# Top-k attention and mixture of experts: the count comparison of the kth score moves from VectorE to GpSimd

## The chip, the core and the metric

The kernel runs on one core of a Trainium2 chip. Its engines are TensorE (PE, with its weight loads as PEld), VectorE (DVE), ScalarE (ACT), GpSimd (POOL) and SyncE (SP, which here issues DMAs). The metric is the time of one execution on the device, in microseconds (us). The kernel before takes 1193.73 us, the median of three runs (1190.71 to 1193.77).

## The reference

```python
# attention: 8 batches, 8 heads, 576 rows, head size 64
scores = scale * np.matmul(q, k.transpose(0, 1, 3, 2))
kth = np.partition(scores, -top_k, axis=-1)[..., -top_k:-top_k + 1]     # top_k = 32
mask = scores >= kth
scores = np.where(mask, scores, -1000000000.0)
attn = np.exp(scores - np.max(scores, axis=-1, keepdims=True))
attn = attn / (np.sum(attn, axis=-1, keepdims=True) + 1e-09)
x = np.matmul(attn, v)                      # then 4608 rows of 512
# experts: 8 of 512 -> 1024 -> 512, one per row
logits = x @ w_gate + modality_bias[modality_id]
e_idx = np.argmax(logits, axis=1)
gate_w = softmax(logits)[np.arange(N), e_idx]
out[mask] = gate_w[mask, None] * (np.maximum(x[mask] @ w1[e], 0.0) @ w2[e])
```

For each row of 576 scores the 32nd largest one (`kth`) is needed, before the exponentials of the scores at or above it are kept.

## The kernel before

**Tiles and steps.** The 64 heads are taken in 32 pairs of 9 tiles of 128 rows by 576 scores: 288 tiles. The main loop (`for i in range(LAST)`, L1123) is a software pipeline. Step i works on tile i in one stage, on tile i - 1 in the next, and so on, and beside it TensorE gets a share of the expert matmuls for batches that are already routed.

**The stages of a tile.** TensorE makes the scores (`qk`, L384), ScalarE copies them to SBUF as `Ssb` (L389). VectorE takes the 8 largest of each of six pieces of 96 (`cand`, L396), and in the next step the 24 largest of these 48 (`chain`, L407 to L409, into `mg`). GpSimd turns the 24th into a threshold (`below`, `n`, L421). ScalarE takes the sign of each score against it (`sign`, `K`, L428) and, in the accumulator of the same instruction, a count that tells how many scores are larger; the count goes to `n[:, 0, x]`. GpSimd multiplies scores and signs (`pool_y`, `y`, L434), one step behind `sign`, and one step behind that VectorE takes the 8 largest of `y` (`find`, L438) into the last places of `mg`.

**The pick.** For three tiles at once, in every third step, `pick` (L440) gives VectorE three small instructions. `eq` (L445) compares the three counts with nine constants `i9s`, giving ones and zeros in 3 x 9; `jk` (L446) multiplies `eq` with nine candidate values of `mg`; `kth` (L447) adds up, so that the one candidate that fits the count is left. Then VectorE masks: `keep` (`P`, L458), one instruction that compares with `kth`, multiplies with the exponentials `ex` and sums the row. For two of three tiles of the first 48 tiles it is split: VectorE makes a mask (`hide`, `hT`, L465), GpSimd adds it to the scores (`hidden`, L471, whose output has the name `ex`), ScalarE takes the exponential (`masked`, L477).

**What sets the order.** VectorE's order inside a step comes from `arrange` (L949), a small planner with a cost, a delay and an earliest time for each kind of work (`USE`, `FROM`, L27 and L28). GpSimd's order is that of the calls in the loop: in a step `hidden` (if there is one), `gate` (L481, one element of `P` read, so that what follows waits for the mask of the step before), `pool_y`, in one step of nine `fill` (L346, two instructions), scatters of routed rows (`DMA_INDIRECT`, L611 and L826, when there are any), `below` (`n`), and in one step of three `small` (`sm`, L415).

Of the kernel before, what the change touches and what calls it, by code (L numbers as in the profile page):

```python
# [9 lines left out]
FT = mybir.dt.float32  # L10
# [4 lines left out]
OP = mybir.AluOpType  # L15
# [25 lines left out]
LY = KL + 2  # L41
LT = LY + 1
# [35 lines left out]
def kernel(  # L78
# [13 lines left out]
    V, A, G, PE, SP = nc.vector, nc.scalar, nc.gpsimd, nc.tensor, nc.sync  # L92
# [21 lines left out]
    wk = att.enter_context(tc.tile_pool(name="wk", bufs=3))  # L114
# [6 lines left out]
    LD, PR, T = {}, {}, {}  # L121
# [55 lines left out]
    def fiota(name, shape, pattern, base, cm):  # L177
        t = const.tile(shape, FT, name=name)
        G.iota(t, pattern=pattern, base=base, channel_multiplier=cm, allow_small_or_imprecise_dtypes=True)
        return t  # L180

    i9s = fiota("i9s", [128, 3, 9], [[0, 3], [2, 9]], S - 2 * TOPK, 0)
# [160 lines left out]
    def fill(p, bd):  # L343
        for h in range(2):
            r = slice(h * 64, h * 64 + 64)
            G.tensor_scalar(bd[r, :, r], PR[p]["st"][r, :, 1, 512:].bitcast(FT), 1.0, 1.0, op0=OP.mult, op1=OP.mult)  # L346
# [84 lines left out]
    def pool_y(i):  # L431
        t = T[i]
        t["y"] = wk.tile([128, S], FT, name="y", bufs=YB)
        G.tensor_tensor(t["y"], t["S"], t["K"], op=OP.mult)  # L434

    def find(i):
        t = T[i]
        V.max(t["mg"][:, i % 3, 24:32], t["y"])  # L438

    def pick(i):  # L440

        t = T[i]
        eq, v = (wk.tile([128, 3, 9], FT, name=nm, bufs=1) for nm in ("eq", "jk"))
        n = t["n"][:, 0, :]
        return [lambda: V.tensor_tensor(eq, i9s, n[:, :, None].to_broadcast([128, 3, 9]), op=OP.is_equal),  # L445
                lambda: V.tensor_tensor(v, eq, t["mg"][:, :, 23:32], op=OP.mult),  # L446
                lambda: V.tensor_reduce(kth[:, i - 2:i + 1], v, axis=AX.X, op=OP.add)]  # L447

    def expo(i):
# [281 lines left out]
    def expert(s, act, nxt, whole, defer):  # L731
# [111 lines left out]
        if nxt:  # L843
            pick, rows, done, tok = sched(s + 1, whole)
            todo = pick + done + rows + tok
            c, k = len(todo) - 2, (2 if whole else 3) * (1 + o["xt"])
            cut = [min(k * x, c) for x in range(CUT[0])] + [c + 1] * (CUT[1] - CUT[0]) + [c + 2]

            def both(f, a, b):
                f()  # L850
                chore.extend(todo[a:b])
                if not defer:
                    chores()
            n = len(cut) - 1
            return [(c, lambda f=f, a=a, b=b: both(f, a, b), w) for (c, f, w), a, b in zip(main, cut, cut[1:])] + main[n:]
# [14 lines left out]
    def ready(n, whole):  # L870
        pick, rows, done, tok = sched(n, whole)
        for f in pick + done + rows + tok:
            f()
        for g in range(4):
            load_w1(n, g)
        for g in range(4):
            load_w2(n, g)
# [13 lines left out]
    def more_moe():  # L891
# [14 lines left out]
        elif full >= n + 1:  # L906
            now = SL[n - 1] if moe else {"xt": True, "used": [4, 4]}
            if not now["xt"]:
                return
            plan.update(ready=n, go=False)  # L910
            pick, rows, done, tok = sched(n, fits(n))
            free = []

            def begin():
                free.extend(now["used"])
                now["nxt"] = True

            def take(x, g):
                return lambda: weight(lambda: (load_w1, load_w2)[x](n, g)) if g < free[x] else None
            l1 = [take(0, g) for g in range(4)]  # L920
            l2 = [lambda: [take(1, g)() for g in range(4)]]
            go = [lambda: plan.update(go=True)]
            if n == 0:
                held = [lambda: [held_.popleft()() for _ in range(len(held_))]]

                def sent():

                    while sends:
                        sends.popleft()()
                rush.extend(pick + [begin] + done + [PAUSE, sent] + rows + l1[:2] + [PAUSE] + go + held + [l1[2], l1[3], PAUSE, PAUSE] + tok + l2)  # L930
            else:
                begun, rest = ([], go) if moe else (go, [])
                rush.extend(pick + [begin] + rows + rest + l1[:1] + done + [PAUSE, l1[1], l1[2], PAUSE, l1[3]] + l2 + begun + [PAUSE] + tok)
# [8 lines left out]
    def run(kind, fs, *after):  # L942

        ops = []
        for f in fs:
            ops.append(Op(kind if isinstance(kind, str) else kind[len(ops)], f, *(ops[-1:] or after)))
        return ops
# [175 lines left out]
    for i in range(LAST):  # L1123
# [138 lines left out]
        ops, found, got = [], None, None  # L1262
# [5 lines left out]
        if ok(i - LT):  # L1268
            found = Op("find", lambda: find(i - LT))
            ops.append(found)  # L1270
            if (i - LT) % 3 == 2:
                e_, v_, s_ = pick(i - LT)
                e_ = Op("pick", e_)
                v_ = Op("pick", v_, e_, found)
                got = Op("pick", s_, v_)
                ops += [e_, v_, got]
        ops += run("late", lo)
        small_ = []
        quick = 0 <= b1 < FAST and r < 16
# [27 lines left out]
            gate(i - 1 - LR)  # L1307
        if ok(i - LY):
            pool_y(i - LY)
        if j == 4 and p + 1 < NPAIR:  # L1310
            fill(p + 1, qbd[(p + 1) % 2])
        for x in puts:
# [13 lines left out]
        if i == CLOSE:  # L1326
# [7 lines left out]
            wk = att.enter_context(tc.tile_pool(name="tl", bufs=1))  # L1334
# [53 lines left out]
    wk = att.enter_context(tc.tile_pool(name="wkb", bufs=3))  # L1388
# [101 lines left out]
```

## Time and profile before

| what | value |
|---|---|
| median of three runs | 1193.73 us (1190.71 to 1193.77) |
| profiled execution, its own time | 1191.36 us |
| its span | 1189.7 us |
| PE busy | 1150.4 us (97%) |
| DVE busy | 1089.2 us (92%) |
| ACT busy | 981.5 us (83%) |
| POOL busy | 670.6 us (56%) |
| chain that ended last | PE 64%, DVE 23%, ACT 6% of the span |
| granted TensorE clock, mean of the span | 0.995 |

Busy time is the union of an engine's instruction spans. The chain is followed back from the last instruction, at each step to what released it. Attention fills the time to about 1008 us; expert matmuls alone follow.

### The profile page before, as it was taken

How to read it: one execution, taken by the hardware profiler on the slowest of the kernel's cores; microseconds unless marked ns; L12 is line 12 of the kernel's file. 1: busy time of each engine (PE TensorE's matmuls, PEld its weight loads, DVE VectorE, ACT ScalarE, POOL GpSimd, SP SyncE). 2: the span in 40 equal slices, each digit the busy share in tenths (PEclk: the TensorE clock that was granted, in tenths of full speed). 3: DMA queues.
4: the chain of work that ended last, by engine and by line, in shares of the span. 5: the costliest groups of instructions: out<-in, count | busy, mean ns of one | idle time of the engine just before them, and what ended most of it. 6: DMA issues, size and time to landing. Idle time of an engine off the chain costs nothing.

```text
span 1189.7 us, 28032 instructions
## 1 busy us (share of the span) xinstructions
PE 1150.4 (97%) x7902; PEld 904.1 (76%) x7902; DVE 1089.2 (92%) x5474; ACT 981.5 (83%) x2015; POOL 670.6 (56%) x1256
## 2 busy tenths in 40 slices
PE   8889979999999999999999999999999999999998
PEld 6667768777777868777686877778687777589987
DVE  7999999999999999999999899999999999476762
ACT  5999979998889979998999899989999887355653
POOL 6888875555656565566566566557655665221111
PEclk9999999999999999999999999999999999999999
DMA  5663357653677368654785448664765554287750
GB/s 125 161 183 90 89 164 221 191 151 87 169 221 199 86 178 241 170 151 129 199 244 156 129 134 242 168 163 133 204 185 134 173 145 148 71 288 250 245 191 22
DMA packets 204323, 197.09 MB, mean 166 GB/s; under 512 B 104413, under 2 KB 151533, under 8 KB 204160
## 3 DMA queue, kind: packets, MB, share of 16 engines
q1 hardware_dynamic: 196880, 175.92, 53.4%
q0 software_dynamic: 6080, 19.00, 4.4%
q8 instruction: 66, 1.08, 0.4%
q14 instruction: 97, 0.79, 0.2%
q10 hardware_dynamic: 1200, 0.30, 0.1%
HBM read 118.63 MB, written 24.23 MB: 120 GB/s over the span
## 4 chain that ended last, share of the span: by engine, by line
PE 64%; DVE 23%; ACT 6%; issue 2%; DMA 2%; POOL 1%; SPq 0%; POOLq 0%; ACTq 0%; DVEq 0%
PE E L798 11%; PE E L811 11%; PE X L520 10%; PE S L384 8%; PE T L492 7%; DVE cand L396 6%; PE X L1085 5%; PE X L1069 4%; DVE mg L438 4%; DVE P L458 4%; PE E L1069 1%; PE X L318 1%; ACT K L428 1%; ACT Ssb L389 1%; DVE cand L407 1%
## 5 line engine op out<-in xcount | busy, mean ns | idle before, releaser
L396 DVE MAX8 cand<-Ssb 128x8 f32<-128x96 f32 x1728 | 389.5, 245 | 2.1 <-ACT Ssb L389 2.1
L434 POOL TENSOR_TENSOR y<-Ssb,K 128x576 f32<-128x576 f32 x288 | 368.2, 1279 | 8.9 <-ACT K L428 8.6
L428 ACT ACTIVATE K<-Ssb,n 128x576 bf16<-128x576 f32 x288 | 230.0, 799 | 9.2 <-POOL y L434 9.0
L384 PE MATMUL S<-ks,qs 128*128 128x288 f32 x992 | 222.7, 346 | 9.9 <-ACT Ssb L389 6.5
L389 ACT ACTIVATE Ssb<-S 128x576 f32<-128x576 f32 x284 | 187.9, 662 | 53.5 <-PE S L384 32.4
L438 DVE MAX8 mg<-y 128x8 f32<-128x576 f32 x288 | 213.4, 741 | 3.9 <-POOL y L434 3.9
L798 PE MATMUL E<-xgT,w1b 128*128 128x256 f32 x832 | 201.2, 384 | 3.5 <-ACT hT L802 1.6
L452 ACT ACTIVATE ex<-Ssb,sm 128x576 f32<-128x576 f32 x256 | 202.9, 793 | 0.0
L500 ACT ACTIVATE PT<-T 128x640 f32<-128x640 f32 (+1 forms) x288 | 193.6, 672 | 6.7 <-PE T L492 6.6
L811 PE MATMUL E<-w2b,hT 128*128 128x512 f32 x416 | 195.8, 597 | 0.5 <-ACT hT L802 0.2
L384 PEld LDWEIGHTS S<-ks,qs 128*128 128x128 f32 x992 | 152.9, 190 | 56.8 <-issue 26.0
L458 DVE SCALAR_TENSOR_TENSOR P<-Ssb,kth,ex 128x576 f32<-128x576 f32 x230 | 191.3, 832 | 3.0 <-ACT ex L452 1.7
L492 PE MATMUL T<-idf,P 128*128 128x128 f32 x1152 | 169.6, 274 | 6.3 <-ACT P L477 5.3
L798 PEld LDWEIGHTS E<-xgT,w1b 128*128 128x128 f32 x832 | 150.8, 190 | 30.0 <-ACT hT L802 6.6
L481 POOL TENSOR_SCALAR spare<-P 1x1 f32<-1x1 f32 x230 | 41.9, 182 | 211.7 <-DVE mg L407 175.0
L492 PEld LDWEIGHTS T<-idf,P 128*128 128x128 f32 x1152 | 137.6, 141 | 12.5 <-ACT P L477 8.8
L520 PE MATMUL X<-PT,vm 128*64 128x256 f32 (+1 forms) x1536 | 145.2, 331 | 1.0 <-ACT xgT L757 0.5
L520 PEld LDWEIGHTS X<-PT,vm 128*64 128x64 f32 x1536 | 87.7, 137 | 45.3 <-issue 10.7
L421 POOL TENSOR_SCALAR n<-mg 128x1 f32<-128x1 f32 x288 | 67.5, 234 | 96.4 <-DVE mg L409 78.9
L811 PEld LDWEIGHTS E<-w2b,hT 128*128 128x128 f32 x416 | 72.6, 190 | 59.6 <-issue 54.7
L428 ACT ACTIVATION_READ_ACCUMULATOR K<-Ssb,n 128x1 f32 x288 | 64.0, 222 | 0.0
L1091 POOL DMA_INDIRECT out_dram<-ot,tk x12 | 12.3, 1026 | 91.0 <-ACT ot L1090 91.0
(223 smaller groups left out, 2146.5 us busy)
## 6 DMA issues: line engine op xcount, KB each, us to landing
w1b<-in_moe_w_dram SPq DMA_DIRECT2D x76, 512.0 KB
w2b<-in_moe_w_dram SPq DMA_DIRECT2D x76, 512.0 KB
ks<-st SPq DMA_DIRECT2D x62, 288.0 KB
ks<-st SPq DMA_DIRECT2D x62, 256.0 KB
qs<-st SPq DMA_DIRECT2D x124, 128.0 KB
xg<-xs SPq DMA_DIRECT2D x19, 516.0 KB
vm<-in_v_dram SPq DMA_DIRECT2D x32, 256.0 KB
km<-in_k_dram SPq DMA_DIRECT2D x63, 128.0 KB
```

The lines of the kernel that those rows point to most:

```text
L384: PE.matmul(ps[:, hf, :288], l, m, start=(n == 0), stop=(n == len(terms) - 1))
L389: A.activation(sb.rearrange("p (a b) -> p a b", a=2), T[i]["ps"], AF.Copy, scale=0.125)
L396: return [lambda s=s: V.max(c[:, s * 8:s * 8 + 8], T[i]["S"][:, bnd[s]:bnd[s + 1]]) for s in range(NSUB)]
L428: A.activation(t["K"], t["S"], AF.Sign, scale=2.0 ** -24 - 1.0, bias=t["n"][:, 1, i % 3:i % 3 + 1], accum_out=t["n"][:, 0, i % 3:i % 3 + 1])
L434: G.tensor_tensor(t["y"], t["S"], t["K"], op=OP.mult)
L438: V.max(t["mg"][:, i % 3, 24:32], t["y"])
L452: A.activation(t["ex"], t["S"], AF.Exp, bias=t["s"][:, i % 3:i % 3 + 1])
L458: V.scalar_tensor_tensor(t["P"], t["S"], kth[:, i:i + 1], t["ex"], op0=OP.is_ge, op1=OP.mult, accum_out=dn)
L492: PE.transpose(T[i]["pt"][:, x, :], (Pm if c == 4 else Pb[c % 2])[:, h * 512 + x * 128:h * 512 + x * 128 + 128], idf)
L520: PE.matmul(o.rearrange("p (a b) -> p a b", a=2) if j < 8 else o, l, r, start=(c == 0), stop=(c == 4))
L798: PE.matmul(ps[:, f % 2], w1b[:, c, f * 128:(f + 1) * 128], xgT[:, c, :], start=(c == 0), stop=(c == KC - 1))
L811: PE.matmul(o["py"], hT[:, f, t * 128:(t + 1) * 128], w2b[:, f, :], start=(f == 0), stop=(f == FC - 1))
```

## The change

A new function `which_count` makes the comparison on GpSimd, 9 constants against the one count of one tile, directly behind that tile's `pool_y`. So there are 288 comparisons of 128 x 9 on GpSimd in place of 96 of 128 x 27 on VectorE. `pick` loses its first instruction, and the planner orders what is left. The new tile `eq` has two buffers, each for three tiles.

```diff
+    def which_count(i):
+
+        t = T[i]
+        x = i % 3
+        t["eq"] = T[i - 1]["eq"] if x else wk.tile([128, 3, 9], FT, name="eq", bufs=2)
+        G.tensor_scalar(t["eq"][:, x, :], i9s[:, x, :], t["n"][:, 0, x:x + 1], 1.0, op0=OP.is_equal, op1=OP.mult)
+
     def pick(i):
 
         t = T[i]
-        eq, v = (wk.tile([128, 3, 9], FT, name=nm, bufs=1) for nm in ("eq", "jk"))
-        n = t["n"][:, 0, :]
-        return [lambda: V.tensor_tensor(eq, i9s, n[:, :, None].to_broadcast([128, 3, 9]), op=OP.is_equal),
-                lambda: V.tensor_tensor(v, eq, t["mg"][:, :, 23:32], op=OP.mult),
+        eq, v = t["eq"], wk.tile([128, 3, 9], FT, name="jk", bufs=1)
+        return [lambda: V.tensor_tensor(v, eq, t["mg"][:, :, 23:32], op=OP.mult),
                 lambda: V.tensor_reduce(kth[:, i - 2:i + 1], v, axis=AX.X, op=OP.add)]
...
-                e_, v_, s_ = pick(i - LT)
-                e_ = Op("pick", e_)
-                v_ = Op("pick", v_, e_, found)
+                v_, s_ = pick(i - LT)
+                v_ = Op("pick", v_, found)
                 got = Op("pick", s_, v_)
-                ops += [e_, v_, got]
+                ops += [v_, got]
...
         if ok(i - LY):
             pool_y(i - LY)
+            which_count(i - LY)
```

The order on VectorE, from the middle of a step with a pick to its mask, among the first 48 tiles; before:

```order
L396 MAX cand<-Ssb 128x8
L445 TENSOR_TENSOR eq<-i9s,n 128x27
L409 MAX mg<-cand_916 128x8
L396 MAX cand<-Ssb 128x8
L446 TENSOR_TENSOR jk<-eq,mg 128x27
L396 MAX cand<-Ssb 128x8
L447 TENSOR_REDUCE kth<-jk 128x3
L396 MAX cand<-Ssb 128x8
L465 TENSOR_SCALAR hT<-Ssb,kth 128x576
```

and with the change (lines behind `pick` are 5 higher):

```order
L396 MAX cand<-Ssb 128x8
L451 TENSOR_TENSOR jk<-eq,mg 128x27
L409 MAX mg<-cand_924 128x8
L396 MAX cand<-Ssb 128x8
L452 TENSOR_REDUCE kth<-jk 128x3
L396 MAX cand<-Ssb 128x8 x2
L470 TENSOR_SCALAR hT<-Ssb,kth 128x576
```

`jk` stands where `eq` stood, and nothing else of the step has moved.

The order on GpSimd over one group of three steps among the first 48 tiles (two of them with the mask added on GpSimd, output `ex`), and the start of the next group; before:

```order
L471 TENSOR_TENSOR ex<-Ssb,hT 128x576
L434 TENSOR_TENSOR y<-Ssb,K 128x576
L421 TENSOR_SCALAR n<-mg 128x1
L471 TENSOR_TENSOR ex<-Ssb,hT 128x576
L434 TENSOR_TENSOR y<-Ssb,K 128x576
L421 TENSOR_SCALAR n<-mg 128x1
L481 TENSOR_SCALAR spare<-P_120 1x1
L434 TENSOR_TENSOR y<-Ssb,K 128x576
L421 TENSOR_SCALAR n<-mg 128x1
L415 TENSOR_SCALAR sm<-mg 128x3
```

and with the change:

```order
L476 TENSOR_TENSOR ex<-Ssb,hT 128x576
L434 TENSOR_TENSOR y<-Ssb,K 128x576
L445 TENSOR_SCALAR eq<-i9s,n 128x9
L421 TENSOR_SCALAR n<-mg 128x1
L476 TENSOR_TENSOR ex<-Ssb,hT 128x576
L434 TENSOR_TENSOR y<-Ssb,K 128x576
L445 TENSOR_SCALAR eq<-i9s,n 128x9
L421 TENSOR_SCALAR n<-mg 128x1
L486 TENSOR_SCALAR spare<-P_119 1x1
L434 TENSOR_TENSOR y<-Ssb,K 128x576
L445 TENSOR_SCALAR eq<-i9s,n 128x9
L421 TENSOR_SCALAR n<-mg 128x1
```

One comparison stands between each `y` and the `n` behind it. The orders of ScalarE, SyncE and TensorE are the same before and after.

## Rows read from the trace of the kernel before

**Rows 1.** Busy time by stretch: us, then PE, PEld, DVE, ACT, POOL busy (instructions), clock.

```profile
60.00:160.00 100.00, 90.64 (x779) 71.68 (x779) 99.93 (x535) 95.76 (x219) 82.81 (x116) 1.00 0.45 113
567.00:1000.00 433.00, 429.51 (x2866) 328.52 (x2866) 425.30 (x2271) 388.11 (x802) 262.23 (x518) 1.00 0.62 171
```

**Rows 2.** The chain that ended last by line, of 60 to 160 us and of 567 to 1000.

```profile
by line: DVE cand L396 23.7%; DVE mg L438 15.6%; DVE hT L465 8.7%; DVE P L458 8.6%; PE X L520 5.8%; DVE cand L407 4.3%; DVE cand L408 4.3%; DVE mg L409 3.5%; DVE mg L407 3.1%; PE E L973 2.9%; DVE mg L408 2.5%; PE T L492 2.4%; PE S L384 2.2%
...
by line: PE E L811 18.2%; PE E L798 18.0%; PE X L520 14.4%; PE S L384 12.8%; PE T L492 10.9%; DVE cand L396 2.6%; PE X L318 1.8%; DVE P L458 1.7%; issue 1.4%; DVE mg L438 1.3%; ACT Ssb L389 1.2%; ACT K L428 1.2%; PE X L783 1.1%; ACT PT L500
```

**Rows 3.** The same chain in order of time: some of its entries of the comparison (start, us).

```profile
362.63 0.09 DVE eq L445
...
381.55 0.55 DVE eq L445
...
564.37 1.01 DVE eq L445
...
941.77 1.01 DVE eq L445
```

**Rows 4.** The instructions that touch `eq`: durations in ns, least, median and largest.

```profile
L445 DVE TENSOR_TENSOR eq<-i9s,n x96: 156/170/1104, 25.7 to 1008.1; 128x27 f32<-128x27 f32 x96
L446 DVE TENSOR_TENSOR jk<-eq,mg x96: 156/170/229, 26.0 to 1008.3; 128x27 f32<-128x27 f32 x96
```

**Rows 5.** POOL in order of time (start us, duration us, idle before): an `n` of later tiles.

```profile
503.73 0.19 POOL L421 TENSOR_SCALAR n<-mg 128x1 f32<-128x1 f32 x1 [0.23 <-DVE mg L409]
```

**Rows 6.** DVE and POOL in order of time: two comparisons, and what POOL runs meanwhile.

```profile
508.85 1.28 POOL L434 TENSOR_TENSOR y<-Ssb,K 128x576 f32<-128x576 f32 x1 [0.64 <-ACT K L428]
509.53 0.65 DVE L445 TENSOR_TENSOR eq<-i9s,n 128x27 f32<-128x27 f32 x1
...
99.67 0.29 POOL L346 TENSOR_SCALAR qbd<-st 64x128 fp32r<-64x128 f32 x1
99.76 0.23 DVE L445 TENSOR_TENSOR eq<-i9s,n 128x27 f32<-128x27 f32 x1
```

**Rows 7.** POOL in order of time: one group of three steps among the first 48 tiles.

```profile
109.44 0.21 POOL L421 TENSOR_SCALAR n<-mg 128x1 f32<-128x1 f32 x1 [0.47 <-DVE mg L409]
109.72 0.20 POOL L415 TENSOR_SCALAR sm<-mg 128x3 f32<-128x3 f32 x1
...
111.75 1.28 POOL L434 TENSOR_TENSOR y<-Ssb,K 128x576 f32<-128x576 f32 x1
113.12 0.28 POOL L421 TENSOR_SCALAR n<-mg 128x1 f32<-128x1 f32 x1
113.50 1.28 POOL L471 TENSOR_TENSOR ex<-Ssb,hT 128x576 f32<-128x576 f32 x1
114.74 1.28 POOL L434 TENSOR_TENSOR y<-Ssb,K 128x576 f32<-128x576 f32 x1
116.11 0.58 POOL L421 TENSOR_SCALAR n<-mg 128x1 f32<-128x1 f32 x1
```

**Rows 8.** DVE in order of time: the masks of that group, and a later `P`.

```profile
109.94 0.50 DVE L465 TENSOR_SCALAR hT<-Ssb,kth 128x576 bf16<-128x576 f32 x1
112.67 0.69 DVE L465 TENSOR_SCALAR hT<-Ssb,kth 128x576 bf16<-128x576 f32 x1
115.59 1.05 DVE L458 SCALAR_TENSOR_TENSOR P<-Ssb,kth,ex 128x576 f32<-128x576 f32 x1
...
507.07 0.80 DVE L458 SCALAR_TENSOR_TENSOR P<-Ssb,kth,ex 128x576 f32<-128x576 f32 x1
```

**Rows 9.** DVE by line, 30 to 145 us: us busy, mean ns of one.

```profile
L458 DVE SCALAR_TENSOR_TENSOR P<-Ssb,kth,ex 128x576 f32<-128x576 f32 x13 | 13.6, 1047 | 0.0
```

**Rows 10.** POOL and DVE in order of time, beside scatters of routed rows.

```profile
559.19 0.97 POOL L611 DMA_INDIRECT xs<-x,dest  x1 [0.21 <-DVE mg L407]
560.75 1.27 POOL L434 TENSOR_TENSOR y<-Ssb,K 128x576 f32<-128x576 f32 x1
561.26 1.37 DVE L458 SCALAR_TENSOR_TENSOR P<-Ssb,kth,ex 128x576 f32<-128x576 f32 x1
```

## The prediction

> **What bounds the kernel now.** I read first the busy time by stretch, to see which engine has no room in which part; then the chain that ended last, by line in the same parts, to see whose work sets the time there; then the rows of the instruction that moves; then POOL and DVE in order of time around its old and its new place.
>
> From 60 to 160 us DVE is busy 99.93 of 100 us and PE 90.64; from 567 to 1000 us PE is busy 429.51 of 433, DVE 425.30 [rows 1]. The chain says the same: in the first stretch nearly all of its large entries are DVE lines, in the second PE matmuls, with DVE's `cand` at 2.6% [rows 2]. So a DVE instruction taken out pays fully among the first tiles, and later only where the chain runs over DVE. Behind 160 us the comparison stands on the chain 17 times, from 362.63 to 941.77 us, out of some 80 that are made there (one in three of the 240 tiles left), mostly with 0.09 us, four times with more [rows 3].
>
> The second thing to see is that DVE and POOL hold each other up. The comparison usually lasts 0.170 us, but up to 1.104 [rows 4]. The one at 509.53 us lasts 0.65, until 510.18; POOL's `y` had run from 508.85 to 510.13. The one at 99.76 lasts 0.23, until 99.99; POOL's `fill` had run until 99.96 [rows 6]. An instruction of DVE with two inputs waits until the POOL instruction under way has ended. It goes the other way too: of the masks, `hT` at 112.67 lasts 0.69 in place of 0.50, to 113.36, just behind the end of `y` at 113.03, and the `n` that POOL started at 113.12 lasts 0.28 in place of 0.2 and ends at 113.40, with the mask. `P` at 115.59 lasts 1.05 in place of 0.80, because `y` runs to 116.02, and the `n` behind that `y` lasts 0.58, until `P` has ended [rows 7, 8]. The largest instructions of DVE, `cand` and `mg`, show nothing of the kind.
>
> **The change part by part.**
>
> *Removed from DVE:* 96 comparisons. One costs DVE 0.09 us of its sequence, as the chain counts it [rows 3]; its span of 0.17 overlaps its neighbours. `jk` takes its place, again a product of two inputs at the same point of the step, so I let it inherit the waits of `eq`: where `y` or `fill` is still running, `jk` now waits for it.
>
> *Added to POOL:* 288 comparisons of 128 x 9 with a scalar per row. No row shows one. The nearest are `sm` with 128 x 3, 0.20 us [rows 7], and `fill` with 64 x 128, 0.29 [rows 6]. I take 0.20, since 9 elements are nearer to 3, and keep 0.29 as the upper bound. As `sm` starts 0.28 behind the start of `n` [rows 7], a comparison moves what follows by about 0.26.
>
> *Added waits:* the comparison needs the count from ScalarE, which the `y` ahead of it has waited for in effect (same instruction, one step back), and a buffer that `jk` left two groups ago. `jk` needs the comparisons of the step before. I cost these at nothing; cover is one whole step of some 3 us.
>
> *Later tiles, the undisturbed step:* `n` waits there for DVE's `mg`, 0.23 us before the `n` at 503.73 [rows 5]. The comparison fits nearly into that gap and costs nothing; without that gap it would cost its 0.26. A `jk` beside it waits as the `eq` beside `fill` did, at most 0.06 more (0.23 against 0.17), and less for a POOL instruction shorter than `fill`'s 0.29; taken as nothing.
>
> *The first tiles:* here POOL has no gap. Take the group of rows 7. `y` ends at 113.03 and `hT` takes over to 113.36. The comparison now comes in the place of `n` and is held in its stead until 113.40; `n` follows, and the next addition starts at 113.76, not 113.50. The `y` behind it then ends at 116.28, not 116.02. `P` has stood since 115.59 waiting for just that end, so it ends 0.26 later: DVE itself loses 0.26. Behind `P` the same happens again: comparison, then `n`, then `gate`, then the `y` of the step with the pick, which now ends some 0.25 later in its step and so overlaps the place of `jk`; that wait I take as 0.06, as beside `fill`. The group pays +0.26 + 0.06 - 0.09 = +0.23. With `fill` in the step (one group in three) its two instructions move back by some 0.5 and end beside the first `hT`, which waits for them: between nothing and one `fill` of 0.29 more, taken as 0.24. Between 30 and 145 us there are 13 groups with such a `P`, 1.047 us in the mean [rows 9]; with one in three, four of them have `fill`. Sum: 9 x 0.23 + 4 x 0.47 = 4.0 us slower. DVE bounds this stretch, and neither engine has room behind it to make it good [rows 1].
>
> *Later tiles on the chain:* 17 x 0.09 = 1.5 us gained. This is also the most that can be gained there as long as the waits stay, since the rest of the chain stays as it is.
>
> *Beside scatters of routed rows:* POOL has no gap there either: in the pattern of rows 10 `y` comes late, `P` waits for it (1.37 in place of 0.80), and the comparison of the next step waits 1.01 on the chain [rows 3, 10]. Two or three comparisons in front move that `y` by 0.52, and the next by 0.26 more, 0.8 in all. Six such stretches show an `eq` of over a microsecond; two of them (564 and 941 us) lie on the chain: 2 x 0.8 = 1.6 us slower. Bounds: nothing, and 6 x 0.8 = 4.8.
>
> **Sum:** + 4.0 - 1.5 + 1.6 = + 4.1 us. The profiled execution took 1191.36 us, so 1195.5; the median of the three runs lies 2.4 higher at 1193.73, and against it the forecast is 1197.8 us, 0.34% slower. About 0.3% (3.6 us) is what a measurement can tell from no change, so the forecast lies at that edge.
>
> **The rivals.**
>
> *The comparison is longer on POOL than its neighbours.* Comparing with a scalar from memory may take twice what DVE takes: 2 x 0.17 = 0.34. It decides from about 0.25 on, where it outlasts the holds by `hT` and the place of `jk`: `y` and comparison then end 1.73 + 0.25 or later into the step. At 0.34 each of the 13 groups loses about 0.1 more (+1.4), and `jk` waits about 0.09 in every undisturbed step, which eats the 1.5. Sum + 4.0 + 1.4 + 1.6 = + 7.0, 1200.7 us. For it: no row has a comparison or a scalar per row on POOL. Against it: all of POOL's small ones lie at 0.2 or under when nothing holds them.
>
> The Trainium skill speaks for this rival and against the change: "GPSIMD Engine Reference", section "Key points", says that for elementwise work VectorE is structurally about twice as fast. By that rule the comparison would take the 0.34 of this rival and the time would be 1200.7; in the trace, `sm` at 0.20 against DVE's 0.17 is far from twice, so I give it the smaller chance.
>
> *Not slower: `jk` does not wait as `eq` did.* Then the four long entries on the chain go as well: 0.46 + 0.48 + 2 x 0.92 = 2.8 us (of 0.55, 0.57 and 1.01 each, less 0.09) [rows 3]. It ends at + 4.1 - 2.8 = + 1.3, 1195.0 us, within 0.3%. It decides where the wait came from the comparison's own operands and not from its form. For it: `jk` was never longer than 0.229 [rows 4]. Against it: it always ran after `eq` had waited, and `P` and `hT` show the same waits.
>
> *Faster: POOL's order gives way.* If the held comparison and `n` went through together, the additions would not move and the first 13 groups would gain 13 x 0.09 = 1.2. With 1.5 and 2.8 that is - 5.5, 1188.2 us. Against it: POOL's small instructions start one by one in the rows, 0.28 apart [rows 7].
>
> **How the numbers follow.** Forecast 0.45, longer comparison 0.2, no wait of `jk` 0.27, faster 0.08. The range leaves out the fourth and the far ends of the scatter bound: from 1192.0 (the third rival with no cost beside scatters and first tiles somewhat cheaper) to 1202.5 (the first rival with another 1.8 of scatter cost). Slower by over 0.3%: all of the first rival and somewhat over half of the forecast, as its sum lies just past the edge, 0.48; within 0.3%: the rest of the forecast, and the third, 0.45; faster 0.07.
>
> **What would show it.** Right: POOL's `eq` at about 0.2 us when not held; in the first 48 tiles the second `hT` as before, `P` some 0.25 longer at 1.3, and a group 9.5 us long in place of 9.2; `jk` with single durations near 1 us; the later pattern of undisturbed steps shorter by 0.09 in three. Wrong: a `P` of 1.05 as before among the first tiles takes away the whole loss; a `jk` never above 0.23 takes away the inherited waits; a gain of more than 1.5 us behind 360 us would say that the chain misled me about who sets the time there.

## The result, and the profile after

| what | before | after |
|---|---|---|
| median of the runs | 1192.22 us (1189.94 to 1193.8, 6 runs) | 1205.19 us (1203.95 to 1208.47, 6 runs) |
| span of the profiled execution | 1189.7 us | 1202.3 us |
| chain that ended last | PE 64%, DVE 23% | PE 50%, DVE 39% |

The changed kernel is slower: ratio 1.0115, 95% interval 1.0095 to 1.0134. The medians lie 13.0 us apart, the spans 12.6. The forecast was + 4.1 us: the sign was right, the size was not, and the time lies above the range.

From the page of the changed kernel, the busy time of the engines and the chain by engine:

```profile
PE 1153.9 (96%) x7902; PEld 904.4 (75%) x7902; DVE 1093.2 (91%) x5378; ACT 982.0 (82%) x2015; POOL 784.3 (65%) x1544
...
PE 50%; DVE 39%; ACT 5%; issue 2%; POOL 2%; DMA 1%; SPq 0%; POOLq 0%; DVEq 0%
```

DVE has 96 instructions fewer and is busy 4.0 us longer than before (1093.2 against 1089.2): it doesn't work longer, it is held longer inside its instructions. POOL has 113.7 us more (784.3 against 670.6). The busy time by stretch, with the columns of [rows 1]:

```profile
60.00:160.00 100.00, 87.12 (x718) 67.35 (x717) 99.29 (x482) 88.92 (x202) 91.19 (x137) 0.97 0.41 105
...
567.00:1000.00 433.00, 426.42 (x2869) 325.45 (x2869) 418.34 (x2204) 384.58 (x799) 314.53 (x644) 1.00 0.61 169
```

In the first tiles DVE finishes 482 instructions in 100 us where it finished 535 (some 11 of the 53 are the comparisons taken out), while it counts as busy all the time. The granted clock of 0.97 in that stretch is not what costs the time: from 80 to 140 us it is 1.00 before and after, and the groups of three there are lengthened as much as the others. The instructions that touch `eq`, to be held beside [rows 4]:

```profile
L445 POOL TENSOR_SCALAR eq<-i9s,n x288: 323/333/838, 18.1 to 1019.3; 128x9 f32<-128x9 f32 x144
...
L451 DVE TENSOR_TENSOR jk<-eq,mg x96: 156/170/1229, 25.1 to 1020.7; 128x27 f32<-128x27 f32 x96
```

A comparison takes POOL 0.33 us, and `jk` now has the long waits that `eq` had on DVE (1.229 at most, as against 0.229 before).

**Where the time went.** Every third step ends its pick with `kth`, so the start of the same `kth` in two traces says how far one kernel is behind the other. The `kth` of the 1st, the 16th (the last of the first tiles) and the 95th pick, before:

```profile
26.28 0.16 DVE L447 TENSOR_REDUCE kth<-jk 128x3 f32<-128x27 f32 x1
...
174.39 0.16 DVE L447 TENSOR_REDUCE kth<-jk 128x3 f32<-128x27 f32 x1
...
1000.84 0.18 DVE L447 TENSOR_REDUCE kth<-jk 128x3 f32<-128x27 f32 x1
```

and after:

```profile
25.52 0.16 DVE L452 TENSOR_REDUCE kth<-jk 128x3 f32<-128x27 f32 x1
...
183.51 0.17 DVE L452 TENSOR_REDUCE kth<-jk 128x3 f32<-128x27 f32 x1
...
1012.82 0.18 DVE L452 TENSOR_REDUCE kth<-jk 128x3 f32<-128x27 f32 x1
```

So the changed kernel is 9.1 us behind at the 16th pick, loses 2.9 more up to 1013 us, and 0.6 behind. At the 1st pick it is 0.8 ahead; that much is the start of the execution (experiments 1 and 6, which change nothing there, stand between 0.5 ahead and 0.1 behind at that place), so from the 1st pick to the 16th it loses 9.9. POOL and DVE of the changed kernel in order of time: the group that answers to [rows 7, 8], then a group with `fill`, then an undisturbed later pick.

```profile
117.11 1.28 POOL L434 TENSOR_TENSOR y<-Ssb,K 128x576 f32<-128x576 f32 x1
118.37 0.54 POOL L445 TENSOR_SCALAR eq<-i9s,n 128x9 f32<-128x9 f32 x1
118.99 0.19 POOL L421 TENSOR_SCALAR n<-mg 128x1 f32<-128x1 f32 x1
119.26 1.28 POOL L476 TENSOR_TENSOR ex<-Ssb,hT 128x576 f32<-128x576 f32 x1
120.50 1.28 POOL L434 TENSOR_TENSOR y<-Ssb,K 128x576 f32<-128x576 f32 x1
121.88 0.71 POOL L445 TENSOR_SCALAR eq<-i9s,n 128x9 f32<-128x9 f32 x1
...
118.03 0.68 DVE L470 TENSOR_SCALAR hT<-Ssb,kth 128x576 bf16<-128x576 f32 x1
...
120.94 1.45 DVE L463 SCALAR_TENSOR_TENSOR P<-Ssb,kth,ex 128x576 f32<-128x576 f32 x1
...
124.05 0.36 DVE L451 TENSOR_TENSOR jk<-eq,mg 128x27 f32<-128x27 f32 x1
...
104.33 0.33 POOL L445 TENSOR_SCALAR eq<-i9s,n 128x9 f32<-128x9 f32 x1
104.63 1.02 POOL L346 TENSOR_SCALAR qbd<-st 64x128 fp32r<-64x128 f32 x2
...
105.00 0.50 DVE L470 TENSOR_SCALAR hT<-Ssb,kth 128x576 bf16<-128x576 f32 x1
...
107.73 1.26 DVE L470 TENSOR_SCALAR hT<-Ssb,kth 128x576 bf16<-128x576 f32 x1
...
849.61 0.36 POOL L445 TENSOR_SCALAR eq<-i9s,n 128x9 f32<-128x9 f32 x1
849.68 0.17 DVE L451 TENSOR_TENSOR jk<-eq,mg 128x27 f32<-128x27 f32 x1
850.04 0.17 DVE L452 TENSOR_REDUCE kth<-jk 128x3 f32<-128x27 f32 x1
...
859.35 0.16 DVE L452 TENSOR_REDUCE kth<-jk 128x3 f32<-128x27 f32 x1
```

The mask `hT` at 118.03 ends at 118.71, but the comparison that it held ends at 118.91, 0.20 later. The addition after it starts 0.55 behind the mask (119.26 against 118.71); before it was 0.14 (113.50 against 113.36 [rows 7, 8]). That moves the next `y` by 0.41, and `P`, which waits for it, lasts 1.45 in place of 1.05. The second held comparison likewise ends 0.20 behind `P` (122.59 against 122.39), and `jk` lasts 0.36. So an ordinary group pays 0.40 for `P` and 0.19 for `jk`, and gains some 0.1 by the `eq` taken off DVE; measured from `kth` to `kth`, it is 0.41 to 0.51 longer. Where `fill` stands in the step, it ends 0.15 behind the first `hT` (105.65 against 105.50), so the addition and the `y` of the next step are late as well, the second `hT` of the group lasts 1.26 rather than 0.68, and the group is 1.07 longer. Nine groups of the first kind and four of the second make 9 x 0.46 + 4 x 1.07 = 8.4 of the 9.9 us; the other 1.5 are in the two groups behind them.

The last rows show the hoped-for gain: undisturbed, a pick starts 9.31 us after the one before it (850.04 to 859.35), and the 9.44 of before was 0.13 longer. It is there in most later groups, and yet the kernel loses 2.9 us in that part. The experiments ask why.

### The profile page after: what moved, and what is told of

It is laid out like the page before. It is cut to its first block, busy times and chain, and to the rows that moved or that the text cites. A ratio compares the mean times of both kernels' runs of the same rounds, so it can differ in the third digit from the quotient of the medians.

```text
span 1202.3 us, 28226 instructions
## 1 busy us (share of the span) xinstructions
PE 1153.9 (96%) x7902; PEld 904.4 (75%) x7902; DVE 1093.2 (91%) x5378; ACT 982.0 (82%) x2015; POOL 784.3 (65%) x1544
## 4 chain that ended last, share of the span: by engine, by line
PE 50%; DVE 39%; ACT 5%; issue 2%; POOL 2%; DMA 1%; SPq 0%; POOLq 0%; DVEq 0%
DVE cand L396 11%; PE E L816 9%; PE E L803 8%; PE X L525 8%; DVE mg L438 7%; DVE P L463 6%; PE S L384 5%; PE T L497 5%; PE X L1090 5%; PE X L1074 4%; DVE cand L407 2%; DVE cand L408 2%; DVE mg L409 2%; PE E L1074 1%; DVE hT L470 1%
## 5 line engine op out<-in xcount | busy, mean ns | idle before, releaser
L396 DVE MAX8 cand<-Ssb 128x8 f32<-128x96 f32 x1728 | 378.1, 241 | 1.5 <-ACT Ssb L389 1.5
L384 PE MATMUL S<-ks,qs 128*128 128x288 f32 x992 | 222.4, 346 | 14.9 <-ACT Ssb L389 12.2
L463 DVE SCALAR_TENSOR_TENSOR P<-Ssb,kth,ex 128x576 f32<-128x576 f32 x230 | 196.9, 856 | 4.3 <-ACT ex L457 2.2
L445 POOL TENSOR_SCALAR eq<-i9s,n 128x9 f32<-128x9 f32 x288 | 108.8, 378 | 1.9
L421 POOL TENSOR_SCALAR n<-mg 128x1 f32<-128x1 f32 x288 | 74.6, 259 | 43.8 <-DVE mg L409 18.3
```

The source lines that it names most:

```text
L384: PE.matmul(ps[:, hf, :288], l, m, start=(n == 0), stop=(n == len(terms) - 1))
L396: return [lambda s=s: V.max(c[:, s * 8:s * 8 + 8], T[i]["S"][:, bnd[s]:bnd[s + 1]]) for s in range(NSUB)]
L463: V.scalar_tensor_tensor(t["P"], t["S"], kth[:, i:i + 1], t["ex"], op0=OP.is_ge, op1=OP.mult, accum_out=dn)
```

## The experiments

My theory: the first tiles lose because DVE's masks hold comparisons that are longer than the hold, and the later part loses beside scatters, where POOL has no room. Rivals: the new order of DVE costs the time, whatever POOL does; POOL's comparison costs at every place alike.

Each edit is shown against the changed kernel (against the kernel before where it says so). Where one execution stands alone, without an interval, only its first tiles are read: the later parts vary from execution to execution (the three of experiment 5 lose 2.9 to 4.6 us behind the first tiles, though nothing is changed there). So whether the later part gains or loses is judged by the times of several executions, and where it does by groups that are longer in the profiles of several kernels.

**1. The later tiles alone on POOL.**

```diff
 def which_count(i):
...
+    if not (i >= 51):
+        return
...
 def pick(i):
...
+    return ([] if i >= 51 else
+            [lambda: V.tensor_tensor(eq, i9s, n[:, :, None].to_broadcast([128, 3, 9]), op=OP.is_equal)]) + [
...
```

> Comparison on GpSimd for tiles from 51 on, on VectorE for the tiles before (17 groups). Theory A (two separate losses: about 7.7 us among the first tiles, where GpSimd has no gap, and about 4.5 us net later, beside scatters of routed rows): first tiles as in the kernel before, whole run about 4 to 5 us slower than before, some 1197. Theory B (the loss is made among the first tiles alone, and the later 4.5 us only follow from the shifted timing): no loss later, about 1 to 2 us faster than before, some 1191.

Measured: 1197.32 us (1196.28 to 1198.81), ratio 1.0036, 1.0024 to 1.0049. Up to the 16th pick it is 0.5 us ahead of before (all of that at the 1st pick already), at the 95th 4.3 behind. So the later part does not gain by the change: it loses by itself.

**2. The first 51 tiles alone on POOL.**

```diff
 def which_count(i):
...
+    if not (i < 51):
+        return
...
 def pick(i):
...
+    return ([] if i < 51 else
+            [lambda: V.tensor_tensor(eq, i9s, n[:, :, None].to_broadcast([128, 3, 9]), op=OP.is_equal)]) + [
...
```

> The reverse: GpSimd compares for the first 51 tiles, VectorE from there on. Theory A: about 8 us slower than before, some 1200, reached by 155 us and then kept. Theory B: about 12 to 13 us slower, some 1205, the last 4 to 5 us of it growing between 160 and 1000 us.

Measured: 1203.56 us (1202.28 to 1204.57), ratio 1.0088, 1.0074 to 1.0102. At the 16th pick it is 9.6 us behind, as the changed kernel is (9.1). By the medians (before: 1193.0 in this comparison) the two halves cost 4.3 and 10.6, together 14.9 where the whole change costs 13.0. By the ratios it is 0.36% and 0.88%, together 1.24%, where the whole is 1.15% (0.95 to 1.34): within the interval they add, and the first tiles are the larger share.

**3. No comparison at all.**

```diff
+    eq1 = const.tile([128, 3, 9], FT, name="eq1")
+    V.tensor_scalar(eq1, i9s, float(S - 2 * TOPK), None, op0=OP.is_equal)
...
 def which_count(i):
...
-    t["eq"] = T[i - 1]["eq"] if x else wk.tile([128, 3, 9], FT, name="eq", bufs=2)
-    G.tensor_scalar(t["eq"][:, x, :], i9s[:, x, :], t["n"][:, 0, x:x + 1], 1.0, op0=OP.is_equal, op1=OP.mult)
+    t["eq"] = eq1
```

> The comparison is left out on both engines: a constant picks the first candidate always, so the 24 largest scores are kept; all else as in the changed kernel. This is VectorE's gain alone. If jk inherits the waits that eq had (theory A): 1.5 to 4 us faster than before, jk with durations over 1 us in some steps. If jk does not wait as eq did: 4 to 7 us faster, jk never above 0.25. If VectorE's share of the comparison hardly counts: within 1 us of before.

Measured: 1190.22 us (1188.98 to 1192.08), ratio 0.9977, 0.9968 to 0.9986. This is all that there is to gain from the comparison, even if it cost nothing elsewhere: 2.8 us. At the 1st pick the kernel is 0.8 us ahead, at the 16th 2.2, at the 95th 2.1. So the first tiles give 1.4 us, 0.09 for each of 15 groups, and in this pair of profiles the later ones give nothing. By the medians up to 1.4 us of gain could still lie outside the first tiles. Busy time from 180 to 1000 us of this kernel (columns of [rows 1]):

```profile
180.00:1000.00 820.00, 812.55 (x5489) 625.43 (x5489) 800.20 (x4217) 734.57 (x1524) 495.55 (x968) 1.00 0.63 170
```

PE is busy 812.55 of 820 us, and before it is 812.86: little room to run ahead into. From `kth` to `kth`, of the 79 groups between the 16th pick and the 95th, 61 are shorter than before by more than 0.05, by 8.0 us in all, and 12 are longer, by 8.0. One of those places, POOL and DVE in order of time:

```profile
386.69 1.28 POOL L436 TENSOR_TENSOR y<-Ssb,K 128x576 f32<-128x576 f32 x1 [0.73 <-ACT K L430]
387.32 1.26 DVE L464 SCALAR_TENSOR_TENSOR P<-Ssb,kth,ex 128x576 f32<-128x576 f32 x1
```

POOL stands idle for 0.73 us until ScalarE has the signs, and `P` then waits for the late `y` (1.26 in place of 0.80). DVE was ahead, and gives it back in a wait. That PE sets this pace is argued from its busy time; no run tests it. The instructions that touch `jk`, in the same kernel:

```profile
L452 DVE TENSOR_TENSOR jk<-eq,mg x96: 155/171/1265, 25.1 to 1006.3; 128x27 f32<-128x27 f32 x96
```

With nothing of `eq` left that could be late, `jk` still lasts up to 1.265: the wait belongs to a DVE instruction with two inputs at that place, not to the comparison's operands.

**4. Comparisons that nobody uses.** Against the kernel before, with a tile of its own, `e2`; in the second one the count is replaced by a number. DVE keeps its `eq`.

```diff
+    def extra(i):
...
+        t["e2"] = T[i - 1]["e2"] if x else wk.tile([128, 3, 9], FT, name="e2", bufs=2)
+        G.tensor_scalar(t["e2"][:, x, :], i9s[:, x, :], t["n"][:, 0, x:x + 1], 1.0, op0=OP.is_equal, op1=OP.mult)
...
             pool_y(i - LY)
+            extra(i - LY)
```

> The kernel before, with the 288 GpSimd comparisons added, their result unused; VectorE still makes its own. This is GpSimd's cost alone. Theory A: the 13 us of the change plus VectorE's gain, so 15 to 18 us slower than before, a GpSimd comparison 0.33 us. Rival (the loss comes from jk waiting for GpSimd's result or from the new order on VectorE): clearly less than 13 us, under 8.

```diff
-        G.tensor_scalar(t["e2"][:, x, :], i9s[:, x, :], t["n"][:, 0, x:x + 1], 1.0, op0=OP.is_equal, op1=OP.mult)
+        G.tensor_scalar(t["e2"][:, x, :], i9s[:, x, :], 512.0, 1.0, op0=OP.is_equal, op1=OP.mult)
```

> The kernel before with 288 unused GpSimd comparisons as in extra_count, but against a fixed number in place of the count of each row. Theory A (the scalar read from memory for each row makes the comparison 0.33 us long): about 0.20 us each, and a smaller loss, 4 to 7 us among the first tiles. Rival (the comparison or the nine elements make it long): 0.33 us as before and the same loss, 9 us among the first tiles.

Measured with the count: 1208.45 us (1207.87 to 1210.87), ratio 1.0132, 1.0115 to 1.0149; 15.5 us slower by the medians, and at the 16th pick 9.1 us behind. DVE's order is that of before there, so POOL's instruction alone makes a loss of this size in the first tiles, and the rival in which the new order makes it falls (experiment 3 has the new order and loses nothing). That both kernels stand at 9.1 is in part chance: an ordinary group is 0.53 to 0.71 longer here against 0.41 to 0.51 in the changed kernel, which has the `eq` off DVE, but a group with `fill` only 0.80 to 0.82 against 1.07. There `fill`'s second instruction runs ahead of the first `hT` (105.05 to 105.34, `hT` from 105.35) and isn't held; in the changed kernel DVE comes earlier by its `eq`, and the first `hT` holds it. So in those four groups the comparison and the shorter pick together cost some 0.3 more than the comparison alone. With a number: 1199.86 us (one execution). The line of the comparisons, with the count:

```profile
L445 POOL TENSOR_SCALAR e<-i9s,n x288: 323/333/895, 17.9 to 1023.6; 128x9 f32<-128x9 f32 x144
```

and with a number:

```profile
L445 POOL TENSOR_SCALAR e<-i9s x288: 249/251/813, 18.7 to 1015.8; 128x9 f32<-128x9 f32 x144
```

So of the price of 0.33 us, the scalar that differs by row makes 0.08; with a number it is 0.25, not the 0.20 that was expected. The starts say the same as the spans: undisturbed, the `n` behind starts 0.39 after a comparison with the count (114.61 to 115.00) and 0.31 after one with a number (123.52 to 123.83). The first 14 groups lose 9.1 us in all at the higher price and 6.9 at the lower one. POOL and DVE in order of time at the lower price:

```profile
117.70 0.47 POOL L445 TENSOR_SCALAR e<-i9s 128x9 f32<-128x9 f32 x1
...
117.37 0.68 DVE L472 TENSOR_SCALAR hT<-Ssb,kth 128x576 bf16<-128x576 f32 x1
...
120.28 1.36 DVE L465 SCALAR_TENSOR_TENSOR P<-Ssb,kth,ex 128x576 f32<-128x576 f32 x1
```

Here the held comparison ends 0.12 behind the mask (118.17 against 118.05), and `P` lasts 1.36. With `n` of 0.19 [rows 7] it is 0.04 and 1.05 (one held instruction fewer), at 0.33 it is 0.20 and 1.45. A held instruction thus ends its own price less 0.13 to 0.15 behind the mask, in these three cases.

**5. At which of the three places.** Against the kernel before, one unused comparison per group of the first 51 tiles: in the step with the pick (k = 0), in the next one (k = 1), or in the third (k = 2).

```diff
+    def extra(i):
...
+        if i >= 51 or x != k:
+            return
+        t["e2"] = wk.tile([128, 3, 9], FT, name="e2", bufs=2)
+        G.tensor_scalar(t["e2"][:, x, :], i9s[:, x, :], t["n"][:, 0, x:x + 1], 1.0, op0=OP.is_equal, op1=OP.mult)
```

> The kernel before with one unused GpSimd comparison with the count for each group of the first 51 tiles, behind the y of the step with the pick. GpSimd has a gap behind it, so nothing in two groups of three; with fill in the step it pushes fill beside the first mask hT, some 0.3 us. About 1 to 2 us over the first 14 groups. Rival (every comparison adds its own 0.33 us to the group): 4.5 us.

> The same, behind the y of the second step of each group, where the second mask hT holds GpSimd and the next addition stands behind: that addition, its y and so P end later by the comparison's own time and what it is held. 0.35 to 0.4 us in each of 13 groups, so about 5 us. If a held comparison ends with the mask, as the prediction had it: 0.26 each, 3.4 us.

> The same, behind the y of the third step, where P holds GpSimd: gate and the y of the next step come later, and jk and eq in that step wait for that y. 0.2 to 0.3 us in each of 13 groups, about 3 to 4 us. If the prediction's 0.06 for that wait were right: under 1 us. The three places together should make the 9.1 us that extra_count lost there; if much is missing, the loss needs two of them at once.

Measured: 1196.56, 1199.32 and 1198.46 us (one execution each, beside 1195.04 of before). The first 14 groups lose 0.9, 5.5 and 3.9 us, together 10.2, where all three at once lose 9.1. Of the 3.9, 1.4 fall on the 14th group alone, where DVE waits 1.26 us for PE (`lt`). The first 13 groups lose 0.7, 5.2 and 2.5, together 8.3 against 8.6 of all three at once, so the places add up. (Behind the first tiles the three lose 4.6, 2.9 and 4.6 us more; that is the variation spoken of above.) Of the second step, POOL and DVE:

```profile
116.05 0.54 POOL L447 TENSOR_SCALAR e<-i9s,n 128x9 f32<-128x9 f32 x1
...
116.94 1.28 POOL L480 TENSOR_TENSOR ex<-Ssb,hT 128x576 f32<-128x576 f32 x1
...
118.62 1.45 DVE L467 SCALAR_TENSOR_TENSOR P<-Ssb,kth,ex 128x576 f32<-128x576 f32 x1
```

and of the third:

```profile
107.83 0.72 POOL L447 TENSOR_SCALAR e<-i9s,n 128x9 f32<-128x9 f32 x1
...
110.00 0.36 DVE L454 TENSOR_TENSOR eq<-i9s,n 128x27 f32<-128x27 f32 x1
...
116.72 1.05 DVE L467 SCALAR_TENSOR_TENSOR P<-Ssb,kth,ex 128x576 f32<-128x576 f32 x1
```

The second step's comparison alone gives `P` its whole 1.45, that is 0.40 a group. The third step's leaves `P` at 1.05 and gives the pick's two-input instruction its 0.36. The one in the step with the pick, where POOL has 0.47 us to spare [rows 7], costs nothing in an ordinary group and 0.2 in one with `fill`. A comparison costs by its place, and the rival of equal cost everywhere falls.

**6. The later loss: at the step's end, and away from the scatters.** Both against experiment 1 (later tiles alone). First the comparison stands behind `n` and `sm`, so that it is no longer ahead of the threshold:

```diff
             pool_y(i - LY)
-            which_count(i - LY)
...
+        if ok(i - LY):
+            which_count(i - LY)
```

> As late_only (GpSimd from tile 51 on), but the comparison stands behind n and sm, at the end of GpSimd's step, not ahead of them. Theory A (GpSimd's added time itself makes the later loss, where it has no gap): again 4 us slower than before, 1197. Theory B (the loss comes by way of a later n, then sign, then y): 0 to 1 us slower, 1193 to 1194.

Then VectorE compares for 18 groups as before, three around each of the six stretches with scatters:

```diff
-        if not (i >= 51):
+        if not (i >= 51 and i // 3 not in (27, 28, 29, 39, 40, 41, 51, 52, 53, 63, 64, 65, 75, 76, 77, 87, 88, 89)):
             return
...
```

> As late_only, but VectorE compares for the 18 groups whose comparisons GpSimd would make beside the scatters of routed rows. Theory A as the prediction had it (the later loss is made beside those scatters): 4 us of late_only's loss go, about as before, 1193. Rival (the loss is made in single steps all over, where y is late for another reason): still 2 to 4 us slower.

Measured: behind `n` 1197.18 us (1195.34 to 1201.65), ratio 1.0041, 1.0026 to 1.0056, as much as in experiment 1, so theory B, the loss by way of a later `n`, falls. Away from the scatters 1193.01 us (1190.08 to 1197.92), ratio 0.9999, 0.9985 to 1.0012: the loss is gone, and no gain is seen. Its profiled execution was its slowest, with a wait of 5.9 us for scores near 340 us, so it is judged by its times; of the profile only the list of waits and the groups beside the scatters are used. From 186 to 1000 us, what DVE waited for (us in all, times, longest), later tiles alone:

```profile
DVE lt L592 <- PE X L584: 13.2, 6, 3.0
DVE mg L438 <- POOL y L434: 5.8, 4, 1.5
```

and away from the scatters:

```profile
DVE lt L592 <- PE X L584: 12.8, 6, 3.0
DVE P L468 <- ACT ex L462: 5.0, 6, 2.6
DVE P L468 <- PE T L502: 0.6, 2, 0.5
```

The four waits of `mg` for `y` are in the changed kernel too (5.8 us, 4 times), and neither before nor here. With the comparison behind `n` they are there as well:

```profile
DVE mg L438 <- POOL y L434: 4.8, 4, 1.2
```

One of them, POOL and DVE in order of time, later tiles alone:

```profile
558.44 1.53 POOL L621 DMA_INDIRECT xs<-x,dest  x1 [0.17 <-issue]
...
561.42 0.71 POOL L421 TENSOR_SCALAR n<-mg 128x1 f32<-128x1 f32 x1
...
562.36 1.27 POOL L434 TENSOR_TENSOR y<-Ssb,K 128x576 f32<-128x576 f32 x1
563.62 0.34 POOL L447 TENSOR_SCALAR eq<-i9s,n 128x9 f32<-128x9 f32 x1
564.14 0.97 POOL L621 DMA_INDIRECT xs<-x,dest  x1 [0.17 <-issue]
...
565.74 1.27 POOL L434 TENSOR_TENSOR y<-Ssb,K 128x576 f32<-128x576 f32 x1
...
563.67 0.76 DVE L438 MAX8 mg<-y 128x8 f32<-128x576 f32 x1 [1.46 <-POOL y L434]
...
566.14 1.49 DVE L468 SCALAR_TENSOR_TENSOR P<-Ssb,kth,ex 128x576 f32<-128x576 f32 x1
```

Before, `y` ran from 560.75 to 562.02 in front of this search, and `P` waited for it [rows 10]. Now it starts 1.61 later: the scatter behind the comparison starts later and lasts 1.53 in place of 1.03, and the `n` in front of `y` is held by a `P` (561.27 to 562.08) and lasts 0.71. DVE has nothing to do for 1.46 us, and the next `y` holds the next `P` (1.49). The long `eq` that stood on the chain there, 1.01 at 564.37 [rows 3], is replaced by those two waits. Up to the pick behind that search the two kernels are even (0.06 shorter than before); the groups of three that start with that pick, at 566, 693, 818 and 943 us of the kernel before, are 0.89, 0.89, 0.90 and 1.12 longer, and the one at 302 us, beside an earlier scatter, 0.96. These five make 4.8 us, all that experiment 1 loses between the 16th pick and the 95th; the other groups, shorter and longer, cancel. In the changed kernel the five are longer by 0.87 to 1.11 too, and away from the scatters by no more than 0.06. With the comparison behind `n` it is the groups just before the four that are 1.18 to 1.26 longer.

No version beat the kernel before with the comparison in it; experiment 3, which leaves it out, is the ceiling.

## Why the prediction was right in sign and wrong in size

**The step that failed** is the price: "I take 0.20, since 9 elements are nearer to 3, and keep 0.29 as the upper bound." It is 0.333, above the bound. The neighbour chosen, `sm`, had other work: by experiment 4 the comparison with a number takes 0.25, and the scalar per row adds 0.08. The first rival had 0.34 from doubling DVE's 0.17, and in its price it was right. The Trainium skill, "GPSIMD Engine Reference", section "Key points", has VectorE about twice as fast for elementwise work, and I gave that the smaller chance. The trace has 0.33 against 0.17, but for 9 elements a row against 27 and with 0.08 of it for the scalar, so no run here tests the rule, and that doubling met the price is in part luck.

**First tiles, forecast + 4.0, measured + 9.1** (8.4 in the 13 groups that the sum counted, 1.5 in two more that it left out, and 0.8 less by the start). The mechanism was as described: held behind the mask, addition late, `y` late, `P` waiting for it, then the same for the pick. What followed from the price is larger. "Is held in its stead until 113.40" says that the held comparison ends with the mask. For `n` that holds (0.04 behind); for 0.33 us of work it is 0.20 behind, so `P` lost 0.40 and not 0.26, and `jk` 0.19 and not 0.06. For 0.20, the relation of experiment 4 would give 0.05 to 0.07 behind the mask (an estimate), so the forecast of `P` at 1.3 was near for the price it assumed. For `fill` I took 0.24 on the first `hT` of the group; it is the second `hT` that lasts 0.58 longer (1.26 against 0.68), while the first keeps its 0.50. Per group: 0.46 rather than 0.23, and 1.07 rather than 0.47.

**The first rival** (1200.7) saw that a longer comparison outlasts the holds, but took 0.1 a group for it; against the forecast's groups it was 0.23 and 0.60. It also let `jk` wait 0.09 in every undisturbed step, and there `jk` lasts 0.17 as ever. So its price was right and its time 4.5 us too low.

**Later tiles on the chain, forecast - 1.5, not seen.** The price of 0.09 a pick was right (experiment 3, first tiles), and most later groups are shorter by as much or more. But in the profiles of experiment 3, with no comparison at all, the 95th pick is no further ahead than the 16th: other groups are longer. So the condition "as long as the waits stay" did not hold. That PE had no room is the likely reason, not a shown one, and a gain of up to 1.4 us is not ruled out by the medians.

**Beside scatters, forecast + 1.6, up to 4.8.** The place was right: experiment 6 takes these groups out, and the loss is gone. The size of one stretch was near (0.8 forecast, 0.89 to 1.12 measured), the number of them was not: I counted the two whose `eq` lay on the chain, and five of the six lose. That makes 4.8 us in experiment 1, the upper end that was kept. In the changed kernel itself the later part shows 2.9, in one execution. The mechanism differs in part: I let `y` be 0.8 later and `eq`'s successor wait for it, but `y` was 1.61 later, DVE's search went idle for it, and then `P` waited.

**That `jk` inherits the waits of `eq`**: right (1.229 after, and 1.265 with nothing to compare), so the rival in which it doesn't wait falls. **That a `jk` beside a comparison waits at most 0.06, taken as nothing**: right (0.17 beside a comparison under way at 849.61). **The rival in which POOL's order gives way**: no; comparison and `n` went one after the other.

In sum: 9.1 + 2.9 + 0.6 at the end = 12.6 us of span, where 4.0 - 1.5 + 1.6 was forecast. The 0.6 was not followed up. Open is also why, beside the scatters, one of the six stretches (at 430 us) loses nothing.

## What to carry to other kernels

Before a small instruction is moved to an engine that looks half idle, find its place between that engine's long ones: here one comparison of three cost nothing, and the other two 0.2 to 0.4 us a group, because a held instruction ends later the longer it is, and what others wait for stands behind it. Price it by a row of the same form (a scalar per row isn't a constant), and where none exists, let the range reach past the nearest neighbours. And first leave the work out altogether: here that gained 0.23%, so no move of it could be expected to gain more.

## What the runs showed of the hardware

GpSimd's comparison of 128 x 9 costs 0.25 us with a number and 0.33 with a scalar per row, against 0.17 for 128 x 27 on VectorE. A held GpSimd instruction doesn't end with what held it, but its own time less 0.13 to 0.15 later (0.04, 0.12 and 0.20 behind the mask at 0.19, 0.25 and 0.33). Not every GpSimd instruction under way holds VectorE: a `jk` that starts 0.07 us into a comparison isn't held (0.17), and the comparison takes 0.36 in place of 0.33; beside a `y` the same `jk` waits until it ends, and so did the `eq` beside the short `fill` (0.29) in [rows 6]. Why the comparison doesn't hold it was not tried.
